# The last 64 weight rows of a decode kernel: other partitions, another queue, and the gate and up weights ahead of the first K tile

## The chip, the cores and the metric

The kernel runs on one core of a Trainium2 chip. The metric is the device time of one execution in microseconds; the median of three runs is taken. Before the change it is 1285.78 us (1285.57 to 1286.98).

## What is computed

One decode step, for one token with D = 448 channels. It mixes an attention block A over a cache of 65536 positions with 8 KV heads (two query heads on each, head size 256) and a gated feed-forward block B with F = 1792, by a gate g. Both blocks read the same x.

```python
x = A_x                                                   # 1 x 448
g = sigmoid((x * gate_w).sum(-1))
q = (x @ A_wq) -> 16 heads of 256;  A_wq is 448 x 4096
p = softmax(q k^T / 16) over 65536 positions, head h on KV head h // 2
a = (p @ v) @ A_wo
b = (relu(x @ B_W_gate) * (x @ B_W_up)) @ B_W_down        # 448 x 1792, 448 x 1792, 1792 x 448
out = g * a + (1 - g) * b
```

The caches k and v hold 8 x 65536 x 256 bf16 each, 512 MiB in all; the weights add about 12.5 MB.

## The kernel before

The caches are read once, in tiles of 16384 positions: 128 partitions x 64 KB, 8 MB. There are four K tiles and four V tiles to a head, 32 of each in all. Three buffers (`ring`, 128 x 64 KB each) take the tiles in turn; a tile's load waits until the work on the buffer's former content is done (`freed`, `held`). A K tile is transposed in place by VectorE (L333, eight pieces), multiplied with the query by PE (L345) and goes through maximum and exponential (L459, L461). After the fourth K tile of a head the four parts are put on one maximum, transposed, and used by PE on the V tiles (L376). The last V tile comes in four pieces (L522), with W_o around them (L531); then the product with W_o (L545) and the output.

All work is put into a plan (`_Plan`): each operation has an engine, a key (a due time worked out by hand) and the operations that it depends on. Each engine runs its operations in order of the key. A dependency becomes a wait on a semaphore, in front of the operation, so that everything behind it on that engine waits too. Operations made by `mop` touch one PSUM bank and are put in one order over all engines (`serialize`). The loop at L202 to L214 lists the loads with their durations; the sum of these gives each load its due time (`tL`), and the keys of the work on it come from that.

The head of the kernel: `A_x` and `gate_w` are loaded from ScalarE's queue (L234, L235), all else from SP's. SP issues W_q, K tile 0, W_gate and W_up, then W_down (L441), which waits for the query product `f_q`, since it is put on the place of W_q, and then the K tiles 1 and 2; K tile 2 goes to the buffer of the weights and waits for `f_gu` and `f_dn`. K tile 0 is in `ring[0]`, K tile 1 in `ring[1]`, the weights and then K tile 2 in `ring[2]`.

D = 448 is 3 x 128 + 64. So each of W_q, W_gate and W_up comes in two parts: rows 0 to 383 in one transfer of 128 partitions with three rows in each (L405, L417), and the last 64 rows by `rows64` (L353): on partitions 0 to 63, in eight transfers of eight partitions that are four apart, all on SP's queue. A row has 8192 B in W_q and 3584 B in W_gate and W_up. x is brought onto partitions by PE and VectorE in the same split (L280 to L288), and copied into a wider tile `xw` for the query product (L293). `f_q` (L299) multiplies 16 heads x 3 row groups with full rows and then 16 products with the 64 rows. `f_gu` (L421) does 84 products with full rows and 28 with the 64 rows. The gate g is worked out ahead of both, with one exponential on ScalarE (L272) and one small product on PE (L276).

Of the kernel before, what the change touches and what calls it, by code (L numbers as in the profile page):

```python
# [24 lines left out]
class _Plan:  # L25
# [65 lines left out]
def bass_gated_mix__gqa_block_cached__glu_gated_reglu__decode_kernel(  # L91
# [33 lines left out]
    assert KR == 64 and FT * 128 == F and FT <= 14 and FT % 2 == 0 and D <= 448 and H >= 3  # L125

    es = ExitStack()
    with es:
# [3 lines left out]
        ring = [sb("ring%d" % i, [128, U * DH], BF) for i in range(NRING)]  # L132
# [36 lines left out]
        WB = (R3 + 1) * NQ  # L169
        wf3 = [ring[2][:, WB + i * R3 * F:WB + (i + 1) * R3 * F] for i in range(2)]  # L170
        WB += 2 * R3 * F
        wfh = [ring[2][:, WB + i * F:WB + (i + 1) * F] for i in range(2)]
        assert WB + 2 * F <= U * DH
        wd_sb = ring[2][:, 0:FT * D].rearrange("p (ft d) -> p ft d", ft=FT)

# [39 lines left out]
        t = 3.0  # L215
        tL, issue = {}, []
# [63 lines left out]
        def f_xT(e):  # L280
            for kt in range(R3):
                e.matmul(XT_ps[:, kt:kt + 1], x_row[0:1, kt:NR3:R3], one_t[0:1, 0:1], start=True, stop=True)
            return e.matmul(XT_ps[0:KR, R3:NX], x_row[0:1, NR3:D], one_t[0:1, 0:1], start=True, stop=True)
        x1_ = mop("pe", 0.6, f_xT, [d_x, c_o1])

        def f_xT2(e):
            e.tensor_copy(xT[:, 0:R3], XT_ps[:, 0:R3])
            return e.tensor_copy(xT[0:KR, R3:NX], XT_ps[0:KR, R3:NX])  # L288
        x2_ = mop("dv", 0.7, f_xT2, [x1_])


        xw3 = xw.rearrange("p (kt c) -> p kt c", kt=NX)
        def f_xw(e):  # L293
            e.tensor_copy(xw3[:, 0:R3, 31:160:32], xT[:, 0:R3].unsqueeze(2).to_broadcast([128, R3, 5])[:, :, 0:5])
            return e.tensor_copy(xw3[0:KR, R3:NX, 31:160:32],
                                 xT[0:KR, R3:NX].unsqueeze(2).to_broadcast([KR, 1, 5])[:, :, 0:5])
        q0 = op("dv", 0.9, f_xw, [x2_, c_xw])

        def f_q(e):  # L299
            for j in range(J):  # L300
                for kt in range(R3):
                    e.matmul(QN_ps, xw3[:, kt, 31 - j:159 - j], wq3[:, kt * NQ + j * 256:kt * NQ + (j + 1) * 256],  # L302
                             start=(j == 0 and kt == 0), stop=False, skip_group_check=True)
            for j in range(J):
                ins = e.matmul(QN_ps, xw3[0:KR, R3, 31 - j:159 - j], wqh[0:KR, j * 256:(j + 1) * 256],
                               start=False, stop=(j == J - 1), skip_group_check=True)
            return ins

# [41 lines left out]

        def rows64(sem, t, dst, W):  # L353
            for i in range(8):
                b0 = i % 4 + 32 * (i // 4)
                d_ = dma("sp", t + 0.0001 * i, sem, lambda e, b0=b0: e.dma_start(  # L356
                    dst[b0:b0 + 29:4, :], W[NR3 + b0:NR3 + b0 + 29:4, :]))
            return d_

        l_, qk, smax, aexp, pv, last = {}, {}, {}, {}, {}, {}  # L360
# [42 lines left out]
        for kind, i, t in issue:  # L403
            if kind == "wq":
                l_["wq"] = dma("sp", t, "wq", lambda e: e.dma_start(wq3, A_wq[0:NR3, :].rearrange("(p k) n -> p (k n)", k=R3)))  # L405
# [3 lines left out]
                l_["qn"] = mop("ac", tq + 9, lambda e: e.copy(qn, QN_ps), [l_["q"], d_gw])  # L409
                l_["qt"] = op("dv", tq + 9.5, lambda e: e.transpose(qrep.bitcast(U32), qn.bitcast(U32)), [l_["qn"], x1_])  # L410
                l_["xm"] = op("dv", tq + 9.6, f_xm, [l_["qt"], c_mask, c_xm])
# [2 lines left out]
            elif kind == "gu":  # L414
                a1 = []
                for i_, W in enumerate((B_W_gate, B_W_up)):
                    a1.append(dma("sp", t + 0.01 * i_, "wf%d" % i_, lambda e, W=W, i_=i_: e.dma_start(  # L417
                        wf3[i_], W[0:NR3, :].rearrange("(p k) f -> p (k f)", k=R3))))
                    a1.append(rows64("wfh%d" % i_, t + 0.01 * i_ + 0.005, wfh[i_], W))

                def f_gu(e):  # L421

                    for ft in range(FT):
                        for which in range(2):
                            c = which * 14 + ft
                            for kt in range(R3):
                                e.matmul(GU_ps[:, c:c + 1], wf3[which][:, kt * F + ft:(kt + 1) * F:FT], xT[:, kt:kt + 1],  # L427
                                         start=(c == 0 and kt == 0), stop=False, skip_group_check=True)
                    for ft in range(FT):
                        for which in range(2):  # L430
                            c = which * 14 + ft
                            ins = e.matmul(GU_ps[:, c:c + 1], wfh[which][0:KR, ft:F:FT], xT[0:KR, R3:NX],
                                           start=False, stop=(ft == FT - 1), skip_group_check=True)
# [15 lines left out]
            elif kind == "k":  # L449
# [14 lines left out]
                if t_ == NTH - 1:  # L464
# [13 lines left out]
                    for rd in range(2):  # L478
# [18 lines left out]
                        q = op("ac", tt + 1, f_ev, [p, pv.get((h - 1) * NTH - 1)])  # L497
# [36 lines left out]
        for h in range(H):  # L534
            i = 0 if h < NW else h - (H - 2) + 1
# [71 lines left out]
```

## Time and profile before

| what | value |
|---|---|
| median of the runs | 1285.78 us (1286.98, 1285.57, 1285.78) |
| profiled execution, first to last instruction | 1286.2 us; no other time is recorded for it |
| PE, VectorE, ScalarE, POOL busy | 428.1, 633.2, 61.2, 4.1 us |
| moved by DMA | 549.65 MB, 427 GB/s over the span |
| idle of VectorE ahead of the transposes (L333) | 413.9 us, for K tiles |
| idle of PE ahead of the V products (L376) | 33.0 us, 29.0 of it for V tiles |
| idle of PE ahead of the query product (L302), the gate/up product (L427) | 4.2 us, 17.9 us, for weights |
| GB/s in the first and the last of 40 slices | 398, 279; 398 to 441 in all but the last, and 405 in the last but one |

"Busy" is time in which an engine executes an instruction; the idle time of a group is that just before its instructions, and the name behind it is what ended most of it. SPq and ACTq rows are the issues of transfers by SP's and ScalarE's sequencers. The DMA share of a stretch counts each packet where it starts, so that in a stretch of 2 us it can be over 1.

### The profile page before, as it was taken

What the parts mean: (1) busy time and instruction counts of PE and PEld (TensorE: products, weight loads), DVE (VectorE), ACT (ScalarE), POOL (GpSimd) and SP (SyncE); (2) the same over time, 40 slices, a digit from 0 to 9 for tenths busy, and PEclk for the clock granted to TensorE, in tenths of its full rate; (3) what the DMA queues carried; (4) which work ended last, traced back from release to release, by engine and by line L of the source; (5) the groups of instructions that cost most, each with busy time, mean ns of one, the idle gap of its engine ahead of it and who ended that gap; (6) DMA issues with size and microseconds to landing.
All of it is one profiled execution on the core that took longest, in us unless ns stands there. A gap on an engine that the chain in (4) does not pass through costs nothing.

```text
span 1286.2 us, 9784 instructions
## 1 busy us (share of the span) xinstructions
PE 428.1 (33%) x4525; PEld 156.2 (12%) x4525; DVE 633.2 (49%) x420; ACT 61.2 (5%) x115; POOL 4.1 (0%) x21
## 2 busy tenths in 40 slices
PE   3424322334123432224331233331323323233336
PEld 2301110111001210001110011110101101011111
DVE  2588633465433655434555443555434556334600
ACT  0000000000000000000000000000000000000000
POOL 1000000000000000000000000000000000000000
PEclk9656666656666565666655666655666656666566
DMA  9999999999999999999999999999999999999996
GB/s 398 434 436 431 435 433 431 435 437 433 426 440 431 431 431 433 435 437 433 426 436 437 431 429 435 431 437 432 433 437 426 435 430 433 432 441 429 426 405 279
DMA packets 12750, 549.65 MB, mean 427 GB/s; under 512 B 1379, under 2 KB 3430, under 8 KB 3558
## 3 DMA queue, kind: packets, MB, share of 16 engines
q1 hardware_dynamic: 12706, 549.03, 99.0%
q8 instruction: 35, 0.57, 0.2%
q14 instruction: 5, 0.04, 0.0%
q10 hardware_dynamic: 4, 0.00, 0.0%
HBM read 549.03 MB, written 0.00 MB: 427 GB/s over the span
## 4 chain that ended last, share of the span: by engine, by line
DVE 34%; DMA 31%; another core or an unknown queue 16%; PE 15%; SPq 2%; ACT 1%; issue 1%; ACTq 0%
DVE ring L333 30%; DMA ring<-in_A_k_cache_dram 27%; PE ST L345 7%; PE O L376 6%; DMA ring<-in_A_wo_dram 2%; DMA ring<-in_B_W_up_dram 2%; DVE P_sb L481 1%; SPq L356 1%; SPq L522 1%; DVE nmb L459 1%; PE PT L486 1%; PE M_ps L427 0%; ACT ptp L495 0%; DVE o_sb L387 0%
## 5 line engine op out<-in xcount | busy, mean ns | idle before, releaser
L333 DVE STREAM_TRANSPOSE ring<-ring 128x2048 uint32<-128x2048 uint32 x256 | 565.4, 2275 | 413.9 <-DMA ring<-in_A_k_cache_dram 413.9
L345 PE MATMUL ST<-ring,xm 128*16 128x512 bf16 x2048 | 225.9, 616 | 757.1 <-DVE ring L333 757.1
L345 PEld LDWEIGHTS ST<-ring,xm 128*16 128x16 bf16 x2048 | 61.6, 120 | 907.1 <-DVE ring L333 797.8
L376 PE MATMUL O<-ring,ptp 128*4 128x512 bf16 x2048 | 149.5, 455 | 33.0 <-DMA ring<-in_A_v_cache_dram 29.0
L461 ACT ACTIVATE P_sb<-ST,nmb 128x512 bf16<-128x512 f32 x32 | 45.2, 1414 | 1111.8 <-DVE nmb L459 1111.8
L459 DVE TENSOR_REDUCE nmb<-ST 128x1 f32<-128x512 f32 x32 | 22.1, 689 | 110.4 <-PE ST L345 110.4
L376 PEld LDWEIGHTS O<-ring,ptp 128*4 128x4 bf16 x2048 | 53.7, 99 | 128.3 <-issue 58.1
L387 DVE CAST o_sb<-O 128x512 bf16<-128x512 f32 x8 | 5.5, 692 | 81.9 <-PE O L376 81.9
L481 DVE TENSOR_TENSOR P_sb<-P_sb,hs 128x1024 bf16<-128x1024 bf16 x16 | 18.9, 1222 | 9.1 <-ACT hs L475 9.1
L486 PE MATMUL PT<-identb,P_sb 128*128 128x128 bf16 x128 | 16.5, 310 | 15.5 <-DVE P_sb L481 14.7
L486 PEld LDWEIGHTS PT<-identb,P_sb 128*128 128x128 bf16 x128 | 12.3, 140 | 18.3 <-DVE P_sb L481 18.3
L495 ACT COPY ptp<-PT 128x256 bf16<-128x256 bf16 x32 | 10.4, 375 | 23.0 <-PE PT L486 23.0
L427 PE MATMUL M_ps<-xT,ring 128*128 128x1 bf16 x84 | 5.2, 198 | 17.9 <-DMA ring<-in_B_W_up_dram 17.9
L302 PE MATMUL M_ps<-ring,P_sb 128*128 128x256 bf16 x48 | 8.3, 358 | 4.2 <-DMA ring<-in_A_wq_dram 4.2
L461 ACT ACTIVATION_READ_ACCUMULATOR P_sb<-ST,nmb 128x1 f32 x32 | 8.4, 263 | 0.0
L545 PE MATMUL A_ps<-ring,attnT 128*1 128x448 bf16 x32 | 8.0, 406 | 0.7 <-DMA ring<-in_A_wo_dram 0.6
L410 DVE STREAM_TRANSPOSE ptp<-P_sb 128x128 uint32<-128x128 uint32 x1 | 0.3, 311 | 14.5 <-ACT P_sb L409 14.5
L427 PEld LDWEIGHTS M_ps<-xT,ring 128*128 128x128 bf16 x84 | 5.1, 161 | 18.0 <-issue 18.0
L302 PEld LDWEIGHTS M_ps<-ring,P_sb 128*128 128x128 bf16 x48 | 6.1, 129 | 6.1 <-issue 4.2
L471 PE MATMUL M_ps<-identf,hs 128*2 128x128 f32 x8 | 2.8, 346 | 10.0 <-DVE hs L469 10.0
L473 PE MATMUL M_ps<-mx,nselT 2*128 2x1 f32 x16 | 4.2, 332 | 3.0 <-DVE mx L472 3.0
L507 DVE RECIPROCAL hs<-M_ps 128x2 f32<-128x2 f32 x8 | 1.4, 171 | 7.4 <-PE M_ps L506 7.4
(72 smaller groups left out, 62.9 us busy)
## 6 DMA issues: line engine op xcount, KB each, us to landing
ring<-in_A_v_cache_dram SPq DMA_DIRECT2D x1, 4096.0 KB, 30.3
ring<-in_A_wq_dram SPq DMA_DIRECT2D x1, 3072.0 KB, 10.2
ring<-in_A_wo_dram SPq DMA_DIRECT2D x1, 2688.0 KB, 33.3
ring<-in_A_v_cache_dram SPq DMA_DIRECT2D x1, 2048.0 KB, 22.9
ring<-in_A_v_cache_dram SPq DMA_DIRECT2D x2, 1024.0 KB, 25.8
ring<-in_B_W_down_dram SPq DMA_DIRECT2D x1, 1568.0 KB, 21.6
ring<-in_B_W_gate_dram SPq DMA_DIRECT2D x1, 1344.0 KB, 28.8
ring<-in_B_W_up_dram SPq DMA_DIRECT2D x1, 1344.0 KB, 27.4
```

The lines of the kernel that those rows point to most:

```text
L302: e.matmul(QN_ps, xw3[:, kt, 31 - j:159 - j], wq3[:, kt * NQ + j * 256:kt * NQ + (j + 1) * 256], start=(j == 0 and kt == 0), stop=False, s ...
L333: return lambda e: e.transpose(v, v)
L345: ins = e.matmul(bank[32 * w:32 * w + 16, :], xm[:, x0:x0 + 16], ktv[sl][:, u0:u0 + 16, c, :, r_], start=(b == 0 and c == 0 and r_ == 0), ...
L356: d_ = dma("sp", t + 0.0001 * i, sem, lambda e, b0=b0: e.dma_start(dst[b0:b0 + 29:4, :], W[NR3 + b0:NR3 + b0 + 29:4, :]))
L376: ins = e.matmul(OP[h % 2][32 * g:32 * g + 4, :], ptp[h % 2][:, col:col + 13:4], ring[sl][:, k * 512:(k + 1) * 512], start=(a == 0 and k < ...
L427: e.matmul(GU_ps[:, c:c + 1], wf3[which][:, kt * F + ft:(kt + 1) * F:FT], xT[:, kt:kt + 1], start=(c == 0 and kt == 0), stop=False, skip_g ...
L459: smax[n] = op("dv", tk + 22, lambda e, n=n, NM=NM, t_=t_: e.tensor_reduce(NM[:, t_:t_ + 1], ST[n % 2][:], AX.X, ALU.max, negate=True), [q ...
L461: aexp[n] = op("ac", tk + 23, lambda e, n=n, t_=t_, NM=NM, RS=RS: e.activation(P_sb[:, t_:2048:4], ST[n % 2][:], ACTF.Exp, bias=NM[:, t_:t ...
L481: rsc = op("dv", tt, lambda e, X=X, pb=pb: e.tensor_tensor(pb, pb, X[:, 12:16].unsqueeze(1).to_broadcast([128, 256, 4]), ALU.mult), [h7, a ...
L486: ins = e.transpose(PT[rd][:, s * 128:(s + 1) * 128], P_sb[:, (rd * 8 + s) * 128:(rd * 8 + s + 1) * 128], identb[:, :])
L495: ins = e.copy(dst, src)
L522: dep = dma("sp", t, "vp%d" % i, lambda e, sl=sl, n=n, lo=lo, hi=hi: e.dma_start(ring[sl][:, lo * 256:hi * 256], v_src(n)[:, lo * 256:hi * ...
```

## The change

Three things change, in one diff.

1. The last 64 rows of each weight are split in 48 and 16. The 48 lie on partitions 0 to 23 and 32 to 55, and come in eight transfers of six partitions that are four apart; the 16 lie on partitions 0 to 15 and come in four transfers of four partitions. So there are twelve transfers for each of the three weights in place of eight. Products over the 48 rows run over 56 partitions; the rows between (24 to 31) are set to zero by a memset of partitions 0 to 31 of the target, on VectorE for W_q and on POOL for W_gate and W_up, and x has zeros there. The query product gets 16 products more, the gate/up product 28 more.
2. These transfers are issued by ScalarE: the twelve of W_q ahead of the exponential of the gate, the 24 of W_gate and W_up right behind it. Each lot waits for its memset. The rows of W_q go to `ring[1]`, so that K tile 1 now waits for the query product by its buffer too.
3. W_gate and W_up stand ahead of K tile 0 in the list of loads. The query product is cut in two operations (full rows, then the last 64), and the gate/up product and the product with W_down come, by their keys, ahead of the first scores.

```diff
-    NX = R3 + 1
+    NX = R3 + 2
+    KA = 48
+    KB = D - NR3 - KA
...
-        wqh = ring[2][:, R3 * NQ:(R3 + 1) * NQ]
+        wqa, wqb = ring[1][:, 0:NQ], ring[1][:, NQ:2 * NQ]
...
-        order = [("wq", 0, 8.7), ("k", 0, TILE), ("gu", 0, 7.7), ("wd", 0, 3.8)]
+        order = [("wq", 0, 8.1), ("gu", 0, 7.1), ("k", 0, TILE), ("wd", 0, 3.8)]
...
-        slot, held, freed = {}, {2: ["gu", "dn"]}, {}
+        slot, held, freed = {}, {1: ["q"], 2: ["gu", "dn"]}, {}
...
+        z_q = op("dv", -0.5, lambda e: e.memset(wqa[0:32, :], 0.0))
+        z_f = op("gp", -0.5, lambda e: e.memset(ring[2][0:32, R3 * NQ + 2 * R3 * F:R3 * NQ + 2 * R3 * F + 2 * F], 0.0))
+        c_xT = op("dv", -0.3, lambda e: e.memset(xT[:], 0.0))
...
+        def f_q2(e):
             for j in range(J):
-                ins = e.matmul(QN_ps, xw3[0:KR, R3, 31 - j:159 - j], wqh[0:KR, j * 256:(j + 1) * 256],
+                e.matmul(QN_ps, xw3[0:56, R3, 31 - j:159 - j], wqa[0:56, j * 256:(j + 1) * 256],
+                         start=False, stop=False, skip_group_check=True)
+            for j in range(J):
+                ins = e.matmul(QN_ps, xw3[0:KB, R3 + 1, 31 - j:159 - j], wqb[0:KB, j * 256:(j + 1) * 256],
                                start=False, stop=(j == J - 1), skip_group_check=True)
...
-        def rows64(sem, t, dst, W):
+        def rows64(sem, t, dst, dst2, W, deps):
             for i in range(8):
-                b0 = i % 4 + 32 * (i // 4)
-                d_ = dma("sp", t + 0.0001 * i, sem, lambda e, b0=b0: e.dma_start(
-                    dst[b0:b0 + 29:4, :], W[NR3 + b0:NR3 + b0 + 29:4, :]))
+                b0, r0 = i % 4 + 32 * (i // 4), NR3 + i % 4 + 24 * (i // 4)
+                dma("ac", t + 0.0001 * i, sem, lambda e, b0=b0, r0=r0: e.dma_start(
+                    dst[b0:b0 + 21:4, :], W[r0:r0 + 21:4, :]), deps)
+            for i in range(4):
+                d_ = dma("ac", t + 0.001 + 0.0001 * i, sem, lambda e, i=i: e.dma_start(
+                    dst2[i:i + 13:4, :], W[NR3 + KA + i:NR3 + KA + i + 13:4, :]), deps)
...
-                l_["wqh"] = rows64("wqh", t + 0.01, wqh, A_wq)
+                l_["wqh"] = rows64("wqh", 0.5, wqa, wqb, A_wq, [z_q])
                 tq = tL["wq", 0]
-                l_["q"] = mop("pe", tq, f_q, [l_["wq"], l_["wqh"], q0])
+                l_["qm"] = mop("pe", tq, f_q, [l_["wq"], q0])
+                l_["q"] = mop("pe", tq + 8, f_q2, [l_["qm"], l_["wqh"]])
...
-                    a1.append(rows64("wfh%d" % i_, t + 0.01 * i_ + 0.005, wfh[i_], W))
+                    a1.append(rows64("wfh%d" % i_, 2 + 0.1 * i_, wfa[i_], wfb[i_], W, [z_f]))
...
-                tg = tL["gu", 0]
+                tg = max(tL["gu", 0], tL["wq", 0] + 10)
```

Here `ac` is ScalarE, `dv` VectorE, `gp` POOL, and the number behind it is the key. `f_gu` gets the same split as `f_q2`, with tiles `wfa` and `wfb` on the place behind W_gate and W_up in `ring[2]`.

More of the change, by code (lines that the diff above doesn't have):

```diff
@@ L124, in bass_gated_mix__gqa_block_cached__glu_gated_reglu__decode_kernel @@
     KR = D - NR3
-    assert KR == 64 and FT * 128 == F and FT <= 14 and FT % 2 == 0 and D <= 448 and H >= 3
+    assert KR == 64 and KB == 16 and FT * 128 == F and FT <= 14 and FT % 2 == 0 and D <= 448 and H >= 3
     es = ExitStack()
@@ L167, in bass_gated_mix__gqa_block_cached__glu_gated_reglu__decode_kernel @@
         wq3 = ring[2][:, 0:R3 * NQ]
-        wqh = ring[2][:, R3 * NQ:(R3 + 1) * NQ]
-        WB = (R3 + 1) * NQ
+        wqa, wqb = ring[1][:, 0:NQ], ring[1][:, NQ:2 * NQ]
+        WB = R3 * NQ
         wf3 = [ring[2][:, WB + i * R3 * F:WB + (i + 1) * R3 * F] for i in range(2)]
         WB += 2 * R3 * F
-        wfh = [ring[2][:, WB + i * F:WB + (i + 1) * F] for i in range(2)]
+        wfa = [ring[2][:, WB + i * F:WB + (i + 1) * F] for i in range(2)]
+        WB += 2 * F
+        wfb = [ring[2][:, WB + i * F:WB + (i + 1) * F] for i in range(2)]
         assert WB + 2 * F <= U * DH
@@ L282, in f_xT @@
                 e.matmul(XT_ps[:, kt:kt + 1], x_row[0:1, kt:NR3:R3], one_t[0:1, 0:1], start=True, stop=True)
-            return e.matmul(XT_ps[0:KR, R3:NX], x_row[0:1, NR3:D], one_t[0:1, 0:1], start=True, stop=True)
+            for p0 in (0, 32):
+                c0 = NR3 + (p0 // 32) * 24
+                e.matmul(XT_ps[p0:p0 + 24, R3:R3 + 1], x_row[0:1, c0:c0 + 24], one_t[0:1, 0:1], start=True, stop=True)
+            return e.matmul(XT_ps[0:KB, R3 + 1:NX], x_row[0:1, NR3 + KA:D], one_t[0:1, 0:1], start=True, stop=True)
         x1_ = mop("pe", 0.6, f_xT, [d_x, c_o1])
@@ L301, in f_q @@
                 for kt in range(R3):
[L302 to L303 removed]
+                    ins = e.matmul(QN_ps, xw3[:, kt, 31 - j:159 - j], wq3[:, kt * NQ + j * 256:kt * NQ + (j + 1) * 256],
+                                   start=(j == 0 and kt == 0), stop=False, skip_group_check=True)
+            return ins
+        def f_q2(e):
             for j in range(J):
[L305 removed]
+                e.matmul(QN_ps, xw3[0:56, R3, 31 - j:159 - j], wqa[0:56, j * 256:(j + 1) * 256],
+                         start=False, stop=False, skip_group_check=True)
+            for j in range(J):
+                ins = e.matmul(QN_ps, xw3[0:KB, R3 + 1, 31 - j:159 - j], wqb[0:KB, j * 256:(j + 1) * 256],
                                start=False, stop=(j == J - 1), skip_group_check=True)
@@ L431, in f_gu @@
                             c = which * 14 + ft
-                            ins = e.matmul(GU_ps[:, c:c + 1], wfh[which][0:KR, ft:F:FT], xT[0:KR, R3:NX],
+                            e.matmul(GU_ps[:, c:c + 1], wfa[which][0:56, ft:F:FT], xT[0:56, R3:R3 + 1],
+                                     start=False, stop=False, skip_group_check=True)
+                    for ft in range(FT):
+                        for which in range(2):
+                            c = which * 14 + ft
+                            ins = e.matmul(GU_ps[:, c:c + 1], wfb[which][0:KB, ft:F:FT], xT[0:KB, R3 + 1:NX],
                                            start=False, stop=(ft == FT - 1), skip_group_check=True)
                     return ins
-                tg = tL["gu", 0]
+                tg = max(tL["gu", 0], tL["wq", 0] + 10)
                 l_["gu"] = mop("pe", tg, f_gu, a1 + [x2_])
```

10 lines of the change are left out of this document (5 added, 5 removed).

## The prediction

> **What bounds the kernel now.** I read the share of the DMA engines first, then the last stretch of the span, then the head.
>
> ```profile
> DMA packets 12750, 549.65 MB, mean 427 GB/s; under 512 B 1379, under 2 KB 3430, under 8 KB 3558
> q1 hardware_dynamic: 12706, 549.03, 99.0%
> q8 instruction: 35, 0.57, 0.2%
> ...
> DVE 34%; DMA 31%; another core or an unknown queue 16%; PE 15%; SPq 2%; ACT 1%; issue 1%; ACTq 0%
> ```
>
> The 16 DMA engines are at work 99% of 1286.2 us, so a chain with 34% of VectorE in it does not tell the bound; the DMA does. One engine's rate is 427/16 = 26.7 GB/s. Only idle DMA time can be won, and it lies at the end. First the table by stretches (last three columns: granted clock, DMA share, GB/s), then the DMA queues between 1278 and 1282 us, then PE at the end:
>
> ```profile
> 1252.00:1274.00 22.00, 14.62 (x120) 4.83 (x120) 0.00 (x0) 0.00 (x0) 0.00 (x0) 0.73 1.01 418
> 1274.00:1276.00 2.00, 1.42 (x16) 0.38 (x16) 0.00 (x0) 0.00 (x0) 0.00 (x0) 0.50 0.63 235
> 1276.00:1278.00 2.00, 1.43 (x16) 0.10 (x8) 0.00 (x0) 0.00 (x0) 0.00 (x0) 0.50 0.16 63
> 1278.00:1280.00 2.00, 0.59 (x12) 0.10 (x8) 0.00 (x0) 0.00 (x0) 0.00 (x0) 0.50 0.09 35
> 1280.00:1282.00 2.00, 1.89 (x16) 0.35 (x8) 0.85 (x2) 0.00 (x0) 0.00 (x0) 0.50 0.04 14
> ```
>
> ```profile
> q1 hardware_dynamic: 52, 0.10, 6.3%
> ```
>
> ```profile
> 1274.58 1.88 PE L376 MATMUL O<-ring,ptp 128*4 128x512 bf16 x16 [1.31 <-DMA ring<-in_A_v_cache_dram]
> 1277.02 1.02 PE L376 MATMUL O<-ring,ptp 128*4 128x512 bf16 x8 [0.57 <-DMA ring<-in_A_v_cache_dram]
> 1279.45 1.03 PE L376 MATMUL O<-ring,ptp 128*4 128x512 bf16 x8 [1.41 <-DMA ring<-in_A_v_cache_dram]
> 1280.60 0.91 PE L545 MATMUL A_ps<-ring,attnT 128*1 128x448 bf16 x2
> ...
> 1281.63 2.40 PE L545 MATMUL A_ps<-ring,attnT 128*1 128x448 bf16 x6
> ```
>
> Until 1274 us all engines work. After 1276 us the shares make (0.16 + 0.09 + 0.04) x 2 x 16 = 9 engine-us, and the 6.3% of the second fence is 1/16: **one DMA engine alone** moves the end of the last V pieces and of W_o, while PE waits for each piece. So the end is set by the engine that is furthest behind. Why is it behind? The trace's single DMA packets (start, duration, size, queue) can be followed from packet to packet, because one starts on an engine where the one before ends; each of the 16 then carries exactly 8 rows of each of the 63 full tiles. When each one ends the last full V tile, and what it carried besides:
>
> ```
> engines                  last full V tile   64-row pieces  q8 fetches (16 KB)       q14 fetches (8 KB)
> 5 of the first eight     1243.9 to 1244.5   yes            0                        one each on two of them
> 1 of the first eight     1246.7             yes            0                        three
> 2 of the first eight     1250.2, 1252.3     yes            4, 5
> 2 of the other eight     1240.2, 1240.6     no             0
> 6 of the other eight     1246.5 to 1246.8   no             4 or 5
> ends of all transfers: 1281.2, 1279.0 (the two late ones), 1276.8, then 1275.6 and less
> ```
>
> Two loads add up: the 64 leftover rows of W_q, W_gate and W_up, which ran on eight engines alone, and the instruction fetches of queue 8 (35 by the page), each of which set its engine back by about 1.55 us and which go round eight engines. Two engines have both.
>
> **The change, part by part.**
>
> *Rows off the late engines.* A row triple (8192 + 3584 + 3584 B) takes 15360/26.7 = 0.575 us on an engine; by the packets' pitch (312 ns, 2 x 141 ns) 0.594 us. Today each of the eight carries 8: 4.75 us. Afterwards a transfer has six rows (eight transfers per weight) or four (four per weight). In the trace an eight-row transfer occupied eight engines, one row each, and the one-row transfers of x and gate_w went to one of these eight, which has no such fetch and is not late. I take six rows to go to six of the eight and four to four, counted from the engine of x. The fetches go round in a fixed order in which the two late engines are neighbours and stand next to the other eight, so I take them as the last two of the first eight, which is just what six rows leave out. Then: late engines 0 triples, -4.75 us each; four engines 12 triples, +2.4 us; two unchanged.
>
> [...]
>
> New ends: late ones 1281.2 - 4.75 = 1276.4 and 1274.3; the third stays at 1276.8; a plain one with 12 triples 1244.1 + 2.4 + 28.9 = 1275.4 (28.9 us is what the latest needed from its last V tile to 1281.2). The one with three fetches of queue 14 is undecided: with 12 triples (three places of five, the place of x and the late two being taken) 1246.7 + 2.4 + 28.9 = 1278.0, with 8 it stays at 1275.6. So the last end falls by 1281.2 - 1278.0 = 3.2 us or by 1281.2 - 1276.8 = 4.4 us; the nearer rows do not choose, and I take the middle, 3.8 us. What follows the last transfer does not change.
>
> *SP.* The rows took SP's time ahead of K0:
>
> ```profile
> 0.73 0.39 SPq L405 DMA_DIRECT2D ring<-in_A_wq_dram  x1
> 1.18 5.45 SPq L356 DMA_DIRECT2D ring<-in_A_wq_dram  x8
> 6.66 0.46 SPq L453 DMA_DIRECT2D ring<-in_A_k_cache_dram  x1
> ...
> 23.66 0.33 SPq L441 DMA_DIRECT2D ring<-in_B_W_down_dram  x1
> ```
>
> ```profile
> L356 SPq DMA_DIRECT2D ring<-in_A_wq_dram x8: 623/623/768, 1.2 to 6.0; - x8
> ```
>
> Now SP issues four large transfers by about 2.5 us. That wins nothing: DMA was busy from the first packet on. What matters is that the queue does not run dry before W_down and K1, which wait for q. Fast engines hold W_q 192 KB, W_gate and W_up 168 KB, K0 512 KB, and at 26.7 GB/s from 2 us on they are empty at 2 + 7.4 + 6.4 + 19.6 = 35.4 us.
>
> *ScalarE, VectorE, POOL ahead of q.*
>
> ```profile
> 1.15 0.56 POOL L253 TENSOR_SCALAR identb<-P_sb 128x128 bf16<-128x128 int32 x1
> ...
> 1.43 0.49 DVE L241 MEMSET xm<- 128x516 uint32 x1
> 1.51 1.28 ACT L272 ACT_TABLE_LOAD   x1 [1.51 <-PEq L592]
> ...
> 7.33 0.61 DVE L271 TENSOR_REDUCE gz<-ptp 1x1 f32<-1x448 f32 x1
> ...
> 7.97 0.20 ACT L272 ACTIVATE gz<-gz 1x1 f32<-1x1 f32 x1 [5.18 <-DVE gz L271]
> ...
> 9.37 0.16 DVE L277 COPY gb<-M_ps 128x2 f32<-128x2 f32 x1 [0.67 <-PE M_ps L276]
> ...
> 13.49 8.29 PE L302 MATMUL M_ps<-ring,P_sb 128*128 128x256 bf16 x48 [4.15 <-DMA ring<-in_A_wq_dram]
> ...
> 21.71 1.92 PE L305 MATMUL M_ps<-ring,P_sb 64*128 64x256 bf16 x16
> ...
> 23.67 0.37 ACT L409 CAST P_sb<-M_ps 128x256 bf16<-128x256 f32 x1 [15.50 <-PE M_ps L305]
> ```
>
> The memset of wqa (32 x 4096 bf16, 2048 words) takes 0.49 x 2048/516 = 1.95 us of VectorE; the rows from ScalarE wait for it, until about 2.8 us. Twelve issues of 0.623 us end at 10.3 (the sum that the exponential waits for is there before, 7.94 + 1.95 = 9.9); the table load (in front of the exponential, as now) and the exponential 11.8; gate scalars and PE's small product, 1.4 us after the exponential now (8.17 to 9.53), 13.2. This product stands ahead of the q products in PE's order, so q starts near 13.5 to 14 (today 13.49), needs 8.3 us, then 32 products at 1.92/16 = 0.12 us: 3.8 us. q is done near 26.3, against 23.6 now. W_down and K1 are issued then, 9 us before the fast engines are empty: hidden. Without that cover each us would cost one. The other 24 issues end at 11.8 + 24 x 0.623 = 26.8; the copy of q queues behind them, xm is ready near 29, and K0, after 6.4 us of W_gate and W_up, lands near 42: hidden. POOL's memset (32 x 3584 bf16) has no row; between 1792 words at VectorE's pace (1.7 us) and a POOL product's pace of 0.56 us for 128 columns (3584 columns: 15.7 us) I take 4 us, by the memset row; even 16 us only moves the gate rows by 4 us.
>
> *Order on PE and K2.* The gate/up products (84 in 5.17 us, then 56 instead of 28) come at about 30 to 40 us, the W_down product near 47, ahead of K0's scores.
>
> ```profile
> 42.31 5.17 PE L427 MATMUL M_ps<-xT,ring 128*128 128x1 bf16 x84 [17.85 <-DMA ring<-in_B_W_up_dram]
> ```
>
> ```profile
> 32.78 17.66 DVE L333 STREAM_TRANSPOSE ring<-ring 128x2048 uint32<-128x2048 uint32 x8 [6.78 <-DMA ring<-in_A_k_cache_dram]
> ```
>
> ```profile
> 57.72 0.80 SPq L453 DMA_DIRECT2D ring<-in_A_k_cache_dram  x2
> ```
>
> K2, which waits for that product, goes out near 50 instead of 57.72; the packets show fast engines dry for up to 1.2 us near 60 us. Filling that helps only engines that are not last: between 0 and -1.2 us for the third one, taken as 0. K0's transposes start 9 us later than the 32.78 of now, but they need 17.66 us and K1 and K2 (39 us of DMA at 8192/16 KB per engine and tile) lie in flight behind it.
>
> Sum: -3.8 us, with nothing on the other side. The profiled span, 1286.2, lies 0.4 above the median of 1285.78; from the median: **1282.0 us**.
>
> **Rivals.**
>
> *The late engines are among the four that get 12 rows.* For it: the number of an engine is inferred, not recorded, and the first packets of the two late ones started early in their group. Against: the engine of x is not late. They would get 4 triples more, 2.4 us: 1288.2, **slower** than before, from the point on where one late engine lies in the first four.
>
> *A late engine keeps its eight rows* (it is the fifth or sixth), or a six-row transfer is split otherwise than by rows: the end stays, 1285.8. "It does not do what it says" is this case.
>
> [...]
>
> *Twelve more small transfers cost.* If nothing covered the 0.623 us of each issue, 7.5 us came on top of the gain: 1282.0 + 7.5 = 1289.5. The rows' pitch of 312 ns per 8 KB against 8192/26.7 = 307 says that an engine hardly notices where a row's transfer ends. [...]
>
> **How the numbers follow.** Forecast 0.74 (its own range 1280.6 to 1283.4: last end at 1275.8 to 1278.6); late engine keeps its rows 0.10; late engine gets more 0.08; dry 0.06; overhead 0.02. The range for 8 in 10 takes in the unchanged case: 1280.6 to 1285.8. 0.2% (2.6 us) is about what a measurement of this kernel can tell from no change, so faster means under 1283.2: 0.72, the forecast but for its upper edge; slower means over 1288.4: 0.07, half of the two middle rivals' chance (their times lie on either side of it by what their terms leave open) and a little of the overhead; same 0.21.
>
> **What would show it.** Right: between 1278 and 1282 us no transfers; the end of the last V pieces 3 to 4 us earlier with several engines ending together; W_down issued near 26 us, K2 near 50. Wrong: one engine alone at the end for longer than now (late engines among the four), or a DMA share under 0.9 between 30 and 40 us (dry).

## The result, and the profile after

The changed kernel takes 1307.9 us (median of 4 runs, 1307.07 to 1308.31), against 1286.38 us for the kernel before in the same comparison (4 runs, 1285.57 to 1287.26). The ratio is 1.0164 with a 95% interval of 1.0152 to 1.0177: **slower by 21.5 us**, where 3.8 us less had been forecast.

First the page of the changed kernel: its span, two of its lines in 40 slices of 32.7 us each, and its DMA queues. The share of q1 (SP's queue) was 99.0% before; q10 is ScalarE's queue.

```profile
span 1306.3 us, 9893 instructions
...
DMA  9849999999999999999999999999999999999997
GB/s 410 363 197 446 420 444 424 440 427 436 432 434 430 434 434 434 430 438 427 440 423 442 422 446 420 444 424 440 428 436 430 434 434 430 434 432 432 433 413 293
DMA packets 12750, 549.66 MB, mean 421 GB/s; under 512 B 1379, under 2 KB 3430, under 8 KB 3558
## 3 DMA queue, kind: packets, MB, share of 16 engines
q1 hardware_dynamic: 12322, 548.05, 97.3%
q10 hardware_dynamic: 388, 0.99, 0.2%
```

The same bytes are moved. The one place that differs is the third slice, 65 to 98 us: a 4 among the nines, 197 GB/s. So the loss lies in the head and not at the end, where the prediction had looked. The table by stretches shows it; the columns are the stretch, its length, then busy time (and count) of PE, PEld, DVE, ACT and POOL, granted clock, DMA share, GB/s. Changed kernel first, then the kernel before:

```profile
28.00:44.00 16.00, 5.18 (x24) 2.80 (x21) 1.89 (x10) 0.37 (x1) 0.00 (x0) 0.50 0.99 425
44.00:60.00 16.00, 0.00 (x0) 0.00 (x0) 0.00 (x0) 0.00 (x0) 0.00 (x0) 0.50 0.95 410
60.00:68.00 8.00, 0.53 (x9) 0.56 (x10) 0.00 (x0) 0.00 (x0) 0.00 (x0) 0.50 0.17 72
68.00:83.00 15.00, 13.56 (x148) 9.66 (x146) 6.75 (x5) 0.00 (x0) 0.00 (x0) 0.53 0.01 3
83.00:100.00 17.00, 7.18 (x64) 1.96 (x64) 13.30 (x8) 1.34 (x2) 0.00 (x0) 0.68 1.03 432
```

```profile
60.00:68.00 8.00, 0.00 (x0) 0.00 (x0) 1.92 (x1) 0.00 (x0) 0.00 (x0) 0.52 0.94 401
68.00:83.00 15.00, 3.59 (x32) 0.94 (x32) 15.00 (x8) 0.00 (x0) 0.00 (x0) 0.50 1.02 441
```

The idle DMA time is 8 x 0.83 + 15 x 0.99 = 21.5 us, as a mean over the engines, against 8 x 0.06 = 0.5 us before. The 21.0 us between them account for the loss: the two profiled spans differ by 20.1 us (1306.3 and 1286.2), and the last V pieces move back by 19.9 us (the last such group of PE started at 1279.45 us before):

```profile
1299.31 1.03 PE L395 MATMUL O<-ring,ptp 128*4 128x512 bf16 x8 [1.44 <-DMA ring<-in_A_v_cache_dram]
```

What emptied the stream? PE of the changed kernel over the first 83 us (start, duration; in brackets idle time before it and what ended it):

```profile
14.35 6.82 PE L312 MATMUL M_ps<-ring,P_sb 128*128 128x256 bf16 x48 [0.34 <-DVE gb L284]
25.72 3.57 PE L318 MATMUL M_ps<-ring,P_sb 56*128 56x256 bf16 x16 [4.55 <-DMA ring<-in_A_wq_dram]
29.22 3.59 PE L321 MATMUL M_ps<-ring,P_sb 16*128 16x256 bf16 x16
...
67.47 5.17 PE L447 MATMUL M_ps<-xT,ring 128*128 128x1 bf16 x84 [33.74 <-DMA ring<-in_B_W_up_dram]
...
76.71 5.38 PE L470 MATMUL A_ps<-ring,hT 128*1 128x448 bf16 x14 [0.53 <-DVE hT L463]
```

and SP's queue with, from the waits, what its K transfers stood for (total, times, longest):

```profile
32.84 0.33 SPq L466 DMA_DIRECT2D ring<-in_B_W_down_dram  x1
33.21 65.04 SPq L478 DMA_DIRECT2D ring<-in_A_k_cache_dram  x3
```

```profile
SPq L478 <- PE A_ps L470: 48.5, 1, 48.5
```

Read it backwards. K2 goes into the buffer that W_gate, W_up and W_down occupy, so SP waits 48.5 us for the W_down product, which ends at 76.71 + 5.38 = 82.1 us. That product waits for the gate/up product, which PE could start at 33.7 us and starts at 67.47: 33.7 us for W_up's transfers. (From 67.47 to 82.1 us, that is for nearly 15 us of the hole, PE works through these products; the stream stands still for them only because the rows came so late.) W_up's large transfer was issued at 1.6 us; what is late are its leftover rows, on ScalarE's queue. They were issued in time:

```profile
17.14 2.49 ACTq L375 DMA_DIRECT2D ring<-in_B_W_gate_dram  x4
19.66 5.70 ACTq L372 DMA_DIRECT2D ring<-in_B_W_up_dram  x8
25.39 2.49 ACTq L375 DMA_DIRECT2D ring<-in_B_W_up_dram  x4
```

The last issue ends at 27.9 us. The rows land until 66.2 us. Single DMA packets of the changed kernel show why; this is one engine, each packet starting where the one before ends, to within 4 ns (start us, duration us, bytes, queue):

```
29.176  0.009      4  q10   end marker of a row's transfer
29.182  2.418  65536  q1    one packet of K0
31.596  0.140   3584  q10   one row
31.732  2.418  65536  q1
34.146  0.009      4  q10   its end marker
34.152  2.421  65536  q1
36.570  0.140   3584  q10   the next row
```

On this engine the packets of the two queues follow each other by turns. The row of 0.14 us comes behind one K packet of 2.42 us, its end marker behind another one: 4.97 us from one row to the next (31.596 to 36.570). Six engines show this pattern at that time and the other ten do not. By stretch, counted by their starts, gate and up rows went through: 14 in 16 to 28 us, 42 to 44 us, 22 to 60 us, 3 to 64 us, and the last **47 within 2.2 us**, once SP's queue was empty.

With these two turns for a row, the rest can be counted from the kernel alone. q10 carries 192 rows and 192 end markers (388 packets with the four of x and gate_w), one marker for each row. So each of the 36 small transfers stands for two turns on an engine that it uses: 72 turns on the four engines that are in all of them. SP's queue has at most 8 (W_q) + 16 (W_gate, W_up) + 8 (K0) + 8 (W_down) + 8 (K1) = 48 packets for an engine until K2, and six end markers of its own. That is less than 72, so by this count the last rows land only when SP's queue has run dry, and what they hold up, K2, cannot then be early. The trace fits: the last 47 rows are about 12 on each of the four engines, with their markers 24 turns, and 72 - 24 = 48.

### The profile page after: what moved, and what is told of

The parts are those of the page before. It is cut to its first block, busy times and chain, and to the rows that moved or that the text cites. A ratio compares the mean times of both kernels' runs of the same rounds, so it can differ in the third digit from the quotient of the medians.

```text
span 1306.3 us, 9893 instructions
## 1 busy us (share of the span) xinstructions
PE 434.0 (33%) x4571; PEld 160.1 (12%) x4571; DVE 634.8 (49%) x423; ACT 61.3 (5%) x115; POOL 7.6 (1%) x22
## 4 chain that ended last, share of the span: by engine, by line
DVE 37%; DMA 28%; another core or an unknown queue 16%; PE 14%; ACTq 2%; SPq 1%; ACT 1%; issue 1%
DVE ring L349 34%; DMA ring<-in_A_k_cache_dram 23%; PE ST L361 6%; PE O L395 6%; DMA ring<-in_B_W_up_dram 3%; DMA ring<-in_A_wo_dram 2%; DVE P_sb L506 1%; ACTq L372 1%; SPq L547 1%; DVE nmb L484 1%; PE PT L511 1%; ACTq L375 1%; PE M_ps L447 0%; ACT ptp L520 0%
## 5 line engine op out<-in xcount | busy, mean ns | idle before, releaser
L447 PE MATMUL M_ps<-xT,ring 128*128 128x1 bf16 x84 | 5.2, 198 | 33.7 <-DMA ring<-in_B_W_up_dram 33.7
L470 PE MATMUL A_ps<-ring,hT 128*1 128x448 bf16 x14 | 5.4, 574 | 0.5 <-DVE hT L463 0.5
```

## The experiments

The theory is that of **turns**: the queue of the rows, beside 64 KB packets on SP's, is the whole loss. Rivals: the new order (W_gate and W_up ahead of K0) leaves too little in flight; the new split with its 36 transfers, memsets and second set of products is slow in itself; the late W_q rows (25.72 us above) do it by way of W_down. Each edit is to the changed kernel if nothing else is said. The kernel before ran beside each group; a ratio is against it.

### K0 in pieces of 8 KB a partition

```diff
-                kd = dma("sp", t, "r%d" % sl, lambda e, n=n, sl=sl: e.dma_start(ring[sl][:], k_src(n)), free(("k", n)))
+                for c in range(8 if n == 0 else 1):
+                    c0, c1 = (c * 4096, c * 4096 + 4096) if n == 0 else (0, U * DH)
+                    kd = dma("sp", t + 0.001 * c, ..., ring[sl][:, c0:c1], k_src(n)[:, c0:c1]), free(("k", n)))
```

> The changed kernel, but K tile 0 comes in eight transfers of 8 KB per partition instead of one of 64 KB; all else stays, ScalarE's row transfers too. Theory A (turns): on each DMA engine SP's and ScalarE's queue take turns packet by packet, so that each row of W_gate and W_up and each end marker waits for one 64 KB packet of K0, 2.42 us; with 8 KB packets it waits for 0.31 us, the gate/up product starts at 35 to 45 us instead of 67.5, K2 is issued before 60 us, the DMA share has no hole, and the time is 1281 to 1284 us if taking the rows off the two late engines pays as forecast, 1286 if it does not. Theory B (ScalarE's transfers are slow by themselves, by issue or latency): the product stays near 67 us and the time at 1305 to 1308. Theory C (the order with W_gate and W_up ahead of K0 is to blame): also 1305 to 1308.

Measured: 1286.48 us, ratio 1.000 [0.9991, 1.0009]. The gate/up product on PE, and the stretches that were empty:

```profile
38.20 5.17 PE L447 MATMUL M_ps<-xT,ring 128*128 128x1 bf16 x84 [9.33 <-DMA ring<-in_B_W_up_dram]
```

```profile
60.00:68.00 8.00, 2.99 (x32) 0.94 (x32) 4.96 (x3) 0.00 (x0) 0.00 (x0) 0.71 0.91 393
68.00:83.00 15.00, 4.19 (x40) 0.94 (x32) 14.34 (x8) 1.40 (x2) 0.00 (x0) 0.50 0.99 428
```

The wait for the rows falls from 33.74 to 9.33 us and the hole is gone, with split, queue and order of the change untouched. Only the cut of K0 differs, and with it the length and number of SP's packets: K0 gives 64 instead of 8, so 104 turns for 72.

### Rows issued by SP, in the old order

```diff
-        order = [("wq", 0, 8.1), ("gu", 0, 7.1), ("k", 0, TILE), ("wd", 0, 3.8)]
+        order = [("wq", 0, 8.7), ("k", 0, TILE), ("gu", 0, 7.7), ("wd", 0, 3.8)]
...
-                dma("ac", t + 0.0001 * i, sem, lambda e, b0=b0, r0=r0: e.dma_start(
+                dma("sp", t + 0.0001 * i, sem, lambda e, b0=b0, r0=r0: e.dma_start(
```

> The new split of the rows (48 on partitions 0-23 and 32-55, 16 on 0-15, in sixes and fours) alone: all row transfers on SP's queue again, K0 ahead of W_up and of the gate and up rows; W_gate ahead of the W_q rows so that the engines have work while SP issues these. Balance theory (two late engines lose 4.75 us of rows): no engine alone at the end, the last transfer ends near 1277 instead of 1281, 1281 to 1283 us. Rival (the late engines are not the ones relieved, or the end does not hang on them): 1286 to 1289.

SP also issues W_gate ahead of W_q's rows here. Measured: 1288.02 us, 1.001 [1.0001, 1.0019]. The 20 us are gone, about 1 us stays. PE and the stretch:

```profile
44.89 5.17 PE L447 MATMUL M_ps<-xT,ring 128*128 128x1 bf16 x84 [21.59 <-DMA ring<-in_B_W_up_dram]
...
59.52 2.81 PE L470 MATMUL A_ps<-ring,hT 128*1 128x448 bf16 x14
```

```profile
60.00:68.00 8.00, 2.33 (x13) 0.84 (x10) 0.52 (x2) 1.40 (x2) 0.00 (x0) 0.84 0.79 319
```

The W_down product now stands behind K0's scores in PE's order, so K2 is issued at 62.4 us and the engines stand still for 1.7 us as a mean (share 0.79 over 8 us, against 0.94 before). That is an order made by this edit's own keys; the last experiment does without it. The gain from the new split does not show: the last transfer ends at 1281.0 us here and at 1281.2 before.

### The kernel before, with only the queue of the rows changed

```diff
-                d_ = dma("sp", t + 0.0001 * i, sem, lambda e, b0=b0: e.dma_start(
+                d_ = dma("ac", t + 0.0001 * i, sem, lambda e, b0=b0: e.dma_start(
```

> The kernel before, with nothing changed but the queue of the 64-row transfers: ScalarE issues them, W_q's ahead of the exponential, the gate and up ones behind it. Theory A (turns): 16 gate/up transfers on each of eight engines, two packets each (row and marker), 32 turns against 64 KB packets of 2.42 us = 77 us, less what passes beside the short packets of W_gate and W_up: the gate/up product starts at 50 to 70 us instead of 42.3, K2 is issued that much later, the stream has a hole of 5 to 20 us, and the time is 1290 to 1303. Theories of the order or of the new split: no change, 1286.

Measured: 1294.82 us, 1.0067 [1.0053, 1.008]: slower by 7.5 us by the medians, with the old split, old tiles and old order. The place was not the one expected. PE, SP and the stretch:

```profile
32.89 8.11 PE L302 MATMUL M_ps<-ring,P_sb 128*128 128x256 bf16 x48 [23.30 <-DMA ring<-in_A_wq_dram]
...
45.36 5.17 PE L427 MATMUL M_ps<-xT,ring 128*128 128x1 bf16 x84 [1.69 <-DVE nselT L413]
```

```profile
42.88 0.33 SPq L441 DMA_DIRECT2D ring<-in_B_W_down_dram  x1
```

```profile
28.00:44.00 16.00, 10.22 (x65) 7.56 (x65) 0.68 (x4) 0.37 (x1) 0.00 (x0) 1.00 0.61 249
```

Here W_q's rows stand beside K0, which follows W_q directly on SP's queue. The query product starts at 32.89 us instead of 13.49, W_down and K1 go out at 42.88 instead of 23.66, and the stream is empty before that: 16 x (1 - 0.61) = 6.2 us. The gate and up rows, expected to decide at 50 to 70 us, were there by 45. The theory of turns fits, with another victim.

### The 64 rows of a weight in one transfer from ScalarE

```diff
-    KA = 48
-    KB = D - NR3 - KA
...
+        def rows64(sem, t, dst, W):
+            return dma("ac", t, sem, lambda e: e.dma_start(dst[0:KR, :], W[NR3:D, :]))
```

> ScalarE's queue and the new order (W_gate and W_up ahead of K0) as in the change, but each weight's 64 rows in ONE transfer of 64 partitions (by the trace's habit four rows on each of 16 engines), without the new split. Theory A (turns): only 5 packets per weight and engine, 10 turns of 2.42 us for gate and up: the gate/up product starts at 30 to 45 us, no hole, and since each engine now has 4 row triples instead of 8 or 0, the late ones gain 2.4 us: 1283 to 1284. Theory C (the new order is to blame): 1300 or more. Theory B (ScalarE slow by itself): between, by the number of transfers.

Measured: 1289.57 us, 1.0022 [1.0014, 1.0031]. q10 now carries 244 packets in place of 388: 192 rows and 48 end markers, beside the four of x and gate_w. Spread over sixteen engines that is four rows and one marker of a weight for each, 15 turns in all, and the product is early: there is no hole.

```profile
28.01 5.17 PE L423 MATMUL M_ps<-xT,ring 128*128 128x1 bf16 x84 [1.69 <-DVE nselT L409]
```

All the same it is slower. The packets themselves last longer; they are told with the next two.

### The old split behind ScalarE, with K0 in eight

```diff
+            for i in range(8):
+                b0 = i % 4 + 32 * (i // 4)
+                d_ = dma("ac", t + 0.0001 * i, sem, lambda e, b0=b0: e.dma_start(
+                    dst[b0:b0 + 29:4, :], W[NR3 + b0:NR3 + b0 + 29:4, :]))
```

> As the first experiment (ScalarE issues the rows, W_gate and W_up ahead of K0, K0 in eight transfers of 8 KB per partition), but with the OLD split of the rows: eight transfers of eight partitions per weight. This takes the new split out of the comparison, with no hole in the stream in either. Theory D (one of the two late engines still carries eight row triples under the new split, the other none; gain 0 to 2 us): end of the transfers at 1279 to 1281.5, time 0 to 2 us above the first experiment, that is 1286 to 1288. Theory of the forecast (both late engines relieved, 3.8 us): 3 to 4.5 us above it, about 1290. If turns are what delayed the rows, no hole here either: gate/up product at 35 to 42 us.

Measured: 1286.7 us, 1.0003 [0.9994, 1.0012], beside 1.0000 [0.9991, 1.0009] for the same kernel with the new split. The split that was to relieve the late engines is worth nothing that these runs can tell.

### Ten rows on four engines and two on the others, from ScalarE and from SP

Eight transfers of four rows and two of sixteen for each weight, meant to let engines without instruction fetches carry most, so that all end more nearly together; the first in the kernel of the section above (K0 in eight), the second in the kernel before, on SP's queue.

```diff
-            for i in range(8):
-                b0 = i % 4 + 32 * (i // 4)
+            for i in range(10):
+                b0, st, c = (i % 4 + 32 * (i // 4), 4, 4) if i < 8 else (16 + 32 * (i - 8), 1, 16)
```

> As e5_eight_old_split, but the 64 rows of a weight in eight transfers of four rows and two of sixteen: ten row triples on four engines, two on each of the other twelve, so that no engine with instruction fetches has more than two, whichever they are. Theory D: the worst engine loses at least 6 triples, 3.5 us, against the old split, the end of the transfers comes to 1277 to 1278.5, time 1283.5 to 1285. Rival (the end does not hang on rows per engine): as e5.

> The kernel before with one edit: the 64 rows in eight transfers of four and two of sixteen (ten triples on four engines, two on the others), all from SP's queue in the old order, no 64 KB packets in turns with them. Theory D: the worst engine loses 3.5 us: 1283 to 1285, faster than before by 0.15 to 0.3%. Rival (row balance is worth nothing): 1286 to 1287.5.

Measured: 1289.21 us, 1.0021 [1.0012, 1.003], and 1289.96 us, 1.0026 [1.0016, 1.0037]. Both are slower. The ends did come together: in the first of the two, twelve engines end the last full V tile between 1251.0 and 1253.2 us and the other four between 1245.2 and 1248.4, where before they ended between 1240.2 and 1252.3. But the level rose. From the single packets (mean durations in ns in the head; the last column is the time of all packets of the kernel, end markers left out, over 16 engines):

```
                            24 KB  10752 B  12544 B  us per engine
before                      1027   404      469      1275.0
one transfer of 64 rows     1255   488      473      1279.0
ten and two rows, ScalarE   1015   579      476      1280.4
ten and two rows, SP        1016   477      544      1281.2
128 half rows (below)       1014   406      477      1275.1
```

In the three kernels of the middle lines, in which transfers to 64 or fewer partitions go to all 16 engines, the packets take 4.0 to 6.2 us an engine more than before; 1.7 to 3.2 us of that lies on the packets of the three columns, which belong to other transfers (128, 256 and 128 packets). All three kernels are slower than before, whatever the balance returned. The lengthening is not theirs alone: W_down's packets also took 554 ns in the kernel with only the queue of the rows changed, where they came after an empty stretch; that cost 0.7 us an engine.

### K0 in two pieces

```diff
-                kd = dma("sp", t, "r%d" % sl, lambda e, n=n, sl=sl: e.dma_start(ring[sl][:], k_src(n)), free(("k", n)))
+                for c in range(2 if n == 0 else 1):
+                    c0, c1 = (c * 16384, c * 16384 + 16384) if n == 0 else (0, U * DH)
...
```

> The changed kernel with K0 in two transfers of 32 KB per partition, so that a turn behind K0 costs 1.21 us and not 2.42. Theory A in numbers: four engines need about 48 turns for gate and up rows and markers; K0 gives 17 instead of 9, W_down 9, K1 9, so 13 or more are still left when SP's queue runs dry near 62 us, and only then they pass quickly: the gate/up product still starts at 64 to 67 us, K2 is no earlier, 1303 to 1308. Rival (the rows' delay is simply proportional to the packet length): product near 45 us, hole gone, 1285 to 1292.

Measured: 1308.12 us (2 runs), 1.0167 [1.0149, 1.0186], as slow as the change. PE and the stretch:

```profile
67.29 5.17 PE L447 MATMUL M_ps<-xT,ring 128*128 128x1 bf16 x84 [38.40 <-DMA ring<-in_B_W_up_dram]
```

```profile
60.00:68.00 8.00, 0.71 (x12) 0.74 (x13) 0.00 (x0) 0.00 (x0) 0.00 (x0) 0.50 0.21 88
```

This tells the turns from a general gain by smaller pieces: 16 packets of K0 give 56 turns, still fewer than 72, and the rows are again late until the stream is empty.

### 128 half rows, and these in the new order; the kernel before again

The kernel before, with each of the 64 rows cut in two halves, so that one transfer per weight fills all 128 partitions, as a full tile does. The products use x on even partitions, then on odd ones. The second kernel adds W_gate and W_up ahead of K0; the third is the kernel before, unchanged.

```diff
-            for i in range(8):
...
+            return dma("sp", t, sem, lambda e: e.dma_start(dst, W[NR3:D, :].rearrange("r (h c) -> (r h) c", h=2)))
```

> The kernel before with the 64 rows of each weight cut in halves: 128 half rows on 128 partitions, one transfer per weight on SP's queue in the old order, so that by the trace's habit each of the 16 engines gets eight half rows (four triples) and writes the same eight partitions as in a full tile; x stands on even or odd partitions with zeros between, and the gate/up product gets 28 small products more. Theory D (rows and instruction fetches per engine set the end): the worst engine has 4 triples instead of 8, -2.4 us: 0.10 to 0.20% faster, last transfer 2 us earlier; and the packets of W_gate, W_down and of the rows keep their 404, 469 and about 160 ns. Rival (after the two slower even splits: spreading rows never pays): 0.1 to 0.3% slower.

> As e9_half_rows, with the new order on top: W_gate and W_up ahead of K0, their product and W_down's ahead of K0's scores; all on SP's queue. Theory A (the order itself is harmless, turns made the hole): K2 is issued near 50 us instead of 58, no hole, time as e9 or up to 0.05% faster. Theory C (the order delays K0 and costs time): 0.3% or more slower than e9.

> The kernel before, unchanged, as a second look: the ratio to itself should be 1.000, its runs should again lie in two groups near 1285.5 and 1287.4 us, and if its profiled execution is of the lower group, the last transfer should end about 2 us earlier than in the first profile because the engine with rows and five instruction fetches has four this time. If the groups have another cause, the end of the transfers does not move with the fetches.

Measured: 1285.1 us, 0.9991 [0.9982, 1.0]; 1285.58 us, 0.9993 [0.9984, 1.0002]; 1286.95 us, 1.0002 [0.9993, 1.0011]. The half rows in the old order, SP and the end on PE:

```profile
1.20 0.41 SPq L362 DMA_DIRECT2D ring<-in_A_wq_dram  x1
```

```profile
1276.76 1.02 PE L380 MATMUL O<-ring,ptp 128*4 128x512 bf16 x8 [1.46 <-DMA ring<-in_A_v_cache_dram]
```

and in the new order PE:

```profile
23.81 5.17 PE L431 MATMUL M_ps<-xT,ring 128*128 128x1 bf16 x84 [1.69 <-DVE nselT L417]
...
44.25 5.38 PE L450 MATMUL A_ps<-ring,hT 128*1 128x448 bf16 x14 [11.91 <-DMA ring<-in_B_W_down_dram]
```

One issue of 0.41 us stands for eight of 5.45 us, packets keep their lengths (table above), and the last V pieces come 2.7 us earlier than in the profile of before (1276.76 against 1279.45). The time shows 1.0 us of it, at the edge of what can be told: the profile of before is of a run near 1288 us, about 2 us above the median of 1286.13 beside which the half rows ran, so more than half of the 2.7 us need not be theirs. The new order costs nothing: 0.9993 beside 0.9991, and its gate/up product is the earliest of all. The unchanged kernel gave times in two groups, 1285.6 to 1286.2 and 1287.4 to 1287.9 us with one run between them; its profile is of a run of 1287.66.

### The change with only the queue undone

```diff
-                dma("ac", t + 0.0001 * i, sem, lambda e, b0=b0, r0=r0: e.dma_start(
+                dma("sp", t + 0.0001 * i, sem, lambda e, b0=b0, r0=r0: e.dma_start(
...
-                l_["wqh"] = rows64("wqh", 0.5, wqa, wqb, A_wq, [z_q])
+                l_["wqh"] = rows64("wqh", 11.5, wqa, wqb, A_wq, [z_q])
```

Split, tiles, memsets and order stay; SP issues W_q's rows ahead of K0 and the others behind it, and the keys of the query and the gate/up product are moved to fit.

> The changed kernel with one part undone: the row transfers are issued by SP again (W_q's between W_up and K0, the gate and up ones behind K0), the new split, the memsets, the new order of W_gate, W_up, K0 and of the products stay. Theory A (ScalarE's queue taking turns with 64 KB packets is the whole loss): rows pass in the order of SP's queue, gate/up product at 42 to 46 us, K2 issued at 54 to 60, no hole or one under 2 us, 1286 to 1288. Theory C (the new order is part of the loss): 1290 or more.

Measured: 1286.6 us, 1.000 [0.999, 1.0009]. SP, and PE:

```profile
11.40 0.44 SPq L478 DMA_DIRECT2D ring<-in_A_k_cache_dram  x1
11.88 5.66 SPq L372 DMA_DIRECT2D ring<-in_B_W_gate_dram  x8
```

```profile
44.68 5.17 PE L447 MATMUL M_ps<-xT,ring 128*128 128x1 bf16 x84 [17.64 <-DMA ring<-in_B_W_up_dram]
...
53.92 4.29 PE L470 MATMUL A_ps<-ring,hT 128*1 128x448 bf16 x14 [0.53 <-DVE hT L463]
```

```profile
60.00:68.00 8.00, 3.59 (x32) 0.98 (x32) 8.00 (x5) 0.00 (x0) 0.00 (x0) 0.52 0.88 360
68.00:83.00 15.00, 3.59 (x32) 0.98 (x32) 11.30 (x7) 1.40 (x2) 0.00 (x0) 0.50 1.02 441
```

The gate/up product comes 23 us earlier than in the change, K2 is issued at 58.2 us instead of 82.1, and the hole does not open (8 x 0.12 = 1.0 us of idle, against 0.5 before). So the queue makes the loss, and neither split nor order adds to it that these runs can tell.

## Why the prediction was wrong, point by point

- **The bound.** That DMA sets the time, and that only idle DMA time can be won or lost, held: 21.0 us more of idle engines went with a span 20.1 us longer, 21.5 us between the medians. That such time lay "at the end" alone did not.
- **The step that failed** is in the part on ScalarE, "The other 24 issues end at 26.8", and in the next, "The gate/up products ... come at about 30 to 40 us, the W_down product near 47 ... K2 ... goes out near 50". The issues were right (27.9 us), the landing was taken to follow at once. Measured: products at 67.47 and 76.71, K2 at 82.1. The step counted what each issue costs its engine and each queue that it passes, but not that its packets might come by turns with those of the other queue, as the packets of the change then did. What it leaned on, that an engine hardly notices where a row's transfer ends (312 ns a row), was read from rows that follow one another in one queue; between 64 KB packets of another queue a row took 4.97 us. The two stretches named as signs were the wrong places too: the share is 0.95 and more until 60 us.
- **A dry stream** ahead of W_down was given 0.06. q was done at 32.8 (PE's last product of 29.22 us plus 3.59) and W_down went out at 32.84, in time: the DMA share is 0.99 from 28 to 44 us. The estimate of 26.3 missed by 6.5 us for two reasons: by the same turns the last W_q row ended at 22.7 us and its end marker at 25.2, so PE waited until 25.72; and the last 32 products took 7.2 us instead of 3.8, at a granted clock of 0.50 (1.00 until 22 us). The hole that did open came later, by way of K2, and left the engines idle for 21.5 us as a mean.
- **Rows off the late engines.** The split of a six-row transfer over six engines, which no row of before showed, is seen: six engines take turns between 29.2 and 30.1 us, and in the kernel with K0 in eight two engines carry 8 triples, four 12, and ten none. Which six they are by number no trace records. But in that kernel's packets one of the two engines that keep 8 triples also has four instruction fetches and ends its last V tile at 1250.4 us. So one late engine was relieved and one not: the rival "a late engine keeps its eight rows" was true of half. In the profiled runs the last transfer ends at 1279.2 us, against 1281.2 with the old split in the otherwise equal kernel; but the first profile is of a run of 1286.29 us and the second of one of 1288.03, so the 2.0 us may be the runs' and not the split's. In the two kernels that issue the new split from SP it ends at 1281.0 and 1280.8. The ratios of the pair, 1.0000 and 1.0003, differ by 0.4 us, and each interval reaches about 1.2 us either way. So the term of 3.8 us is not to be seen in any run; at most a small part of it is there.
- **Twelve more small transfers cost**: the 7.5 us do not show. On SP's queue they cost nothing that can be told (1.000 [0.999, 1.0009]).
- **Memsets.** VectorE's took 1.76 us (1.95 forecast), POOL's 3.08 (4 taken). Right, and without consequence.
- **The span and the median.** The profiled run of the changed kernel took 1308.06 us for a span of 1306.3, 1.8 us more; with the unchanged kernel profiled again it was 1287.66 for 1285.9. The span of 1286.2 us before thus belonged to a run near 1288, not to the median of 1285.78 from which the prediction subtracted: it worked on a run of the upper group. The range for the forecast's own case is 0.2 us off besides: last ends of 1275.8 to 1278.6 give 1280.4 to 1283.2 by the step that gives 1282.0.

Open: what makes the two groups of the unchanged kernel. That an instruction fetch more falls on an engine with rows (1.55 us each) would fit in size; the second profile fell in the upper group too, with five fetches on such an engine as the first, so there is nothing to compare with. Why three of the splits slow the packets of others is open as well; the runs show only that the three splits with 16 engines in transfers to 64 or fewer partitions have it, and the others, apart from W_down's packets in one kernel, do not.

## What to carry to other kernels

In these runs small transfers on a second queue did not get past a stream of large packets: a row took two turns on an engine, one for its data and one for its end marker, each behind one packet of the stream (4.97 us a row beside 64 KB packets). Before moving such transfers, count these turns and compare them with the packets that the stream has left before it must wait for them. Here 72 turns stood against 48 and, with K0 in two, 56 packets, and the stream stood still; against 104 it did not. If the turns are more, keep the transfers in the stream's own queue (1286.6 us here, against 1307.9), or shorten the stream's packets while they are in flight (1286.48 us with K0 in eight). Of the cuts of leftover rows tried here, the one in which one transfer fills all 128 partitions cost nothing (0.9991 and 0.9993) and needed one issue for eight, even though the products then need a masked operand.

## What the hardware showed that was not expected

- In the changed kernel the end marker of a row's transfer, 4 bytes and 0.009 us, took a turn of its own: it came 2.41 us after the end of its row, behind a 64 KB packet of 2.42 us.
- In the three kernels whose transfers put rows on 16 engines but on 64 or fewer partitions, packets of other transfers were up to 43% longer (10752 B: 404 before, 579 ns with ten and two rows from ScalarE), and all packets took 4.0 to 6.2 us more over the kernel, as a mean over the engines.
- After the hole in the stream the engines are in step again: K2's first packets start within 0.7 us of each other on all engines (83.1 to 83.8 us). At the last full V tile the engines end in two groups again, 1263.8 to 1266.0 us on eight and 1270.0 to 1270.9 us on the other eight; 32 instruction fetches of queue 8 lie in between, which is four on each of the eight engines that carry them; by the 1.55 us of each in the profile before, 4 x 1.55 = 6.2 us.
